# Moving the batched columns of one softmax half from GpSimd to VectorE in a 64-step recurrent attention kernel

## Chip, cores, metric

One core of a Trainium2 chip. The metric is the device time of one execution in microseconds (us). Engines: PE is the matrix engine (PEld its weight loads), DVE is VectorE, ACT is ScalarE, POOL is GpSimd.

## The reference, cut to what matters

A layer of attention with recurrent memory is followed by a gated MLP. The attention walks 64 segments of 32 rows; eight memory rows of one segment's output are the first rows of the next, so the segments are a chain:

```python
for s in range(n_seg):                        # 64
    h = jnp.concatenate([mem, xs], axis=1)    # 8 + 32 rows
    q, k, v = ...                             # 32 heads of 128
    scores = jnp.einsum('bhqe,bhke->bhqk', q, k) * scale
    scores = jnp.where(mask[None, None], scores, -1000000000.0)
    p = _softmax(scores, axis=-1)
    o = jnp.einsum('bhqk,bhke->bhqe', p, v)
    o = jnp.einsum('bhte,hed->btd', o, Wo)
    mem = o[:, :M, :].copy()
```

## The kernel before

Each step treats the 32 heads in two halves, b = 0 and 1. Per half, the exponentials E have 160 columns for the segment's keys and 64 "batched" columns for the last eight keys, whose keys and values were made ahead for 16 segments at once. R holds the reciprocal sums. Both groups of columns are multiplied by R, then go into the value product. The comments give the line numbers by which the profile names the instructions.

```python
def qx_copy(s):     # L574: batched queries of step s
    ...
    pool(lambda e: e.tensor_copy(out=dst, in_=src), reads=..., writes=[("QTe", 0), ("QTe", 1)])

def sm_ln(b):       # L626
    act(... func=ACT.Ln ..., writes=[("R", b)])
def sm_rcp(b):      # L630
    act(... func=ACT.Exp, scale=-1.0 ..., reads=[("R", b)], writes=[("R", b)])

def sm_norm(b):
    dve(lambda e: e.tensor_tensor(out=E_sb[:, b, 0:160], in0=R_sb[:, b, :], in1=E_sb[:, b, 0:160], op=ALU.mult),   # L634
        reads=[("R", b), ("E", b)], writes=[("E", b)])
    ev = E_sb[:, b, 160:224].rearrange("p (g q) -> p g q", q=16)
    rv = R_sb[:, b, :].rearrange("p (g q) -> p g q", q=40)[:, :, 0:16]
    pool(lambda e: e.tensor_tensor(out=ev, in0=rv, in1=ev, op=ALU.mult),                                           # L638
         reads=[("R", b), ("Ex", b)], writes=[("Ex", b)])

def PV_half(s, b):
    for g in range(4):
        for c in range(4):
            pe(...)     # L666: V x E,  reads=[("V", b, g), ("E", b)]
    for c in range(4):
        pe(...)         # L672: batched V x Ex, stop=True, reads=[("Vx", xb, b), ("Ex", b)]
...
# in a step, from the second half's softmax on
sm_norm(0); sm_sums(1); sm_ln(1); sm_rcp(1)
...
V_evac(1, "dve", (0, 2))      # L658
V_evac(1, "act", (2, 4))      # L656
sm_norm(1)
if s + 1 < NSEG: qx_copy(s + 1)
...                           # filler matmuls; even steps have one group more than odd ones
PV_half(s, 0)
PV_half(s, 1)
...                           # two groups of filler matmuls
cT_evac(...)                  # L686 on ACT, L688 on VectorE: out of PSUM, wait for L672
Wo(WOQ, OB, 0, OC)            # L701: output product, waits for cT_evac
```

Waits are derived from the `reads` and `writes` tokens. Instructions on PE take no waits on earlier PE instructions; every other engine also waits for itself where a token says so, and each GpSimd instruction waits for the one before it.

The softmax here doesn't subtract the row's maximum and nothing guards it: scores larger than these inputs give would overflow.

Of the kernel before, what the change touches and what calls it, by code (L numbers as in the profile page):

```python
# [10 lines left out]
ALU = mybir.AluOpType  # L11
# [167 lines left out]
def fast_path(nc, st, keep, A_x, A_mem0, A_Wq, A_Wk, A_Wv, A_Wo, A_seg_len, B_w_in, B_w_sp, B_b_sp, B_w_out, out):  # L179
# [118 lines left out]
    def dve(fn, **k):  # L298
        return em.add("dve", fn, **k)

    def pool(fn, **k):
        return em.add("pool", fn, **k)
# [330 lines left out]
    def sm_norm(b):  # L633
        dve(lambda e: e.tensor_tensor(out=E_sb[:, b, 0:160], in0=R_sb[:, b, :], in1=E_sb[:, b, 0:160], op=ALU.mult),  # L634
            reads=[("R", b), ("E", b)], writes=[("E", b)])
        ev = E_sb[:, b, 160:224].rearrange("p (g q) -> p g q", q=16)
        rv = R_sb[:, b, :].rearrange("p (g q) -> p g q", q=40)[:, :, 0:16]
        pool(lambda e: e.tensor_tensor(out=ev, in0=rv, in1=ev, op=ALU.mult),  # L638
             reads=[("R", b), ("Ex", b)], writes=[("Ex", b)])

    def V_half(s, b, gs, dc, first=0, last=3, held=False):
# [293 lines left out]
    for s in range(NSEG):  # L935
# [68 lines left out]
        V_half(s, 1, (0, 2), 1, 3, 0)  # L1004
        V_half(s, 1, (0, 2), 0, 3, 0)
        sm_norm(0)
        sm_sums(1)
        sm_ln(1)
# [4 lines left out]
# [3 lines that stand above are left out]
        if s + 1 < NSEG:  # L1016
            qx_copy(s + 1)
# [1041 lines left out]
```

## Time and profile before

| | before |
|---|---|
| time, median of 3 runs (range) | 852.48 us (852.42 to 853.62) |
| profiled run | 850.12 us, span 848.4 us, granted clock 0.999 |
| the 64-step scan | from 52 to about 673 us of the span |
| PE busy | 834.1 us, 98% |
| VectorE, GpSimd busy | 515.3 and 168.7 us |

The prediction below shows the lines themselves. A row of the page's groups reads: line, engine, operation, output<-inputs, count, busy us and mean ns, then idle time before it and what ended it. A timeline line reads: start us, duration us, engine, line, operation, and in brackets the idle time before it. I also used the trace's own records, which carry each start and end, and the moment of each semaphore update, in ns.

### The profile page before, as it was taken

How to read it: one execution, taken by the hardware profiler on the slowest of the kernel's cores; microseconds unless marked ns; L12 is line 12 of the kernel's file. 1: busy time of each engine (PE TensorE's matmuls, PEld its weight loads, DVE VectorE, ACT ScalarE, POOL GpSimd, SP SyncE). 2: the span in 40 equal slices, each digit the busy share in tenths (PEclk: the TensorE clock that was granted, in tenths of full speed). 3: DMA queues.
4: the chain of work that ended last, by engine and by line, in shares of the span. 5: the costliest groups of instructions: out<-in, count | busy, mean ns of one | idle time of the engine just before them, and what ended most of it. 6: DMA issues, size and time to landing. Idle time of an engine off the chain costs nothing.

```text
span 848.4 us, 46072 instructions
## 1 busy us (share of the span) xinstructions
PE 834.1 (98%) x22552; PEld 438.3 (52%) x19480; DVE 515.3 (61%) x1322; ACT 471.7 (56%) x1367; POOL 168.7 (20%) x425
## 2 busy tenths in 40 slices
PE   8889999999999999999999999999999999999998
PEld 8545555555545555555555555555555544444443
DVE  3456666676666666666766666666666664453443
ACT  3446666766667676667666666767666755300000
POOL 7312212121212122221222121122111232100000
PEclk9999999999999999999999999999999999999999
DMA  9972220222332221322222324242321690033001
GB/s 319 392 231 75 69 74 28 60 72 61 77 92 58 50 66 43 75 38 61 60 73 73 95 57 80 60 94 72 58 52 56 188 280 7 1 112 106 32 12 40
DMA packets 112920, 75.25 MB, mean 89 GB/s; under 512 B 70728, under 2 KB 98512, under 8 KB 112720
## 3 DMA queue, kind: packets, MB, share of 16 engines
q1 hardware_dynamic: 111504, 70.88, 30.2%
q8 instruction: 166, 2.72, 1.3%
q0 software_dynamic: 384, 1.05, 0.3%
q10 hardware_dynamic: 832, 0.33, 0.1%
q14 instruction: 34, 0.28, 0.1%
HBM read 39.46 MB, written 20.58 MB: 71 GB/s over the span
## 4 chain that ended last, share of the span: by engine, by line
PE 92%; SPq 5%; DMA 1%; issue 0%; DVE 0%; ACT 0%
PE f_ps L289 33%; PE f_ps L701 14%; PE f_ps L290 12%; PE f_ps L1172 11%; PE f_ps L751 3%; PE f_ps L666 3%; PE f_ps L1165 3%; PE f_ps L1248 3%; SPq L329 3%; PE f_ps L1129 3%; PE f_ps L498 2%; DMA f_arena<-in_A_Wo_dram 1%; SPq L825 1%; PE f_ps L595 1%; PE f_ps L615 1%; PE f_ps L672 1%
## 5 line engine op out<-in xcount | busy, mean ns | idle before, releaser
L289 PE MATMUL f_ps<-f_arena,f_hT 128*32 128x512 bf16 (+1 forms) x5632 | 359.7, 331 | 0.3
L289 PEld LDWEIGHTS f_ps<-f_arena,f_hT 128*32 128x32 bf16 x5632 | 133.1, 96 | 161.6 <-issue 69.8
L290 PE MATMUL f_ps<-f_arena,f_hT 128*32 128x512 bf16 (+1 forms) x2560 | 188.5, 315 | 0.0
L559 ACT ACTIVATE f_Tst<-f_ps 128x512 bf16<-128x512 f32 (+1 forms) x320 | 149.7, 510 | 57.6 <-PE f_ps L289 53.9
L701 PE MATMUL f_ps<-f_arena,f_cT 128*32 128x256 bf16 x4096 | 130.6, 274 | 0.9 <-DMA f_arena<-in_A_Wo_dram 0.6
L638 POOL TENSOR_TENSOR f_E_sb<-f_R_sb,f_E_sb 128x64 bf16<-128x64 f32 x128 | 57.0, 446 | 362.1 <-ACT f_R_sb L630 362.1
L567 DVE STREAM_TRANSPOSE f_QT<-f_Tst 128x256 uint32<-128x256 uint32 x128 | 57.1, 446 | 94.3 <-ACT f_Tst L559 94.3
L701 PEld LDWEIGHTS f_ps<-f_arena,f_cT 128*32 128x32 bf16 x4096 | 90.0, 94 | 37.1 <-ACT f_cT L686 23.2
L1172 PE MATMUL f_ps<-f_arena 128*128 128x512 bf16 x448 | 100.6, 379 | 0.0
L688 DVE TENSOR_SCALAR f_cT<-f_ps 128x160 bf16<-128x160 f32 x256 | 65.2, 318 | 35.2 <-PE f_ps L672 35.2
L713 ACT ACTIVATE f_part<-f_ps 128x256 bf16<-128x256 f32 x128 | 49.1, 383 | 57.7 <-PE f_ps L701 53.7
L658 DVE TENSOR_SCALAR f_V_sb<-f_ps 128x512 bf16<-128x512 f32 (+1 forms) x128 | 71.1, 555 | 13.6 <-PE f_ps L289 13.6
L686 ACT ACTIVATE f_cT<-f_ps 128x160 bf16<-128x160 f32 x256 | 57.1, 310 | 36.3 <-PE f_ps L672 36.3
L1172 PEld LDWEIGHTS f_ps<-f_arena 128*128 128x128 bf16 x448 | 43.8, 98 | 52.8
L567 DVE STREAM_TRANSPOSE f_KT<-f_Tst 128x128 uint32<-128x128 uint32 (+1 forms) x192 | 65.9, 356 | 2.8
L626 ACT ACTIVATE f_R_sb<-f_ps 128x160 f32<-128x160 f32 x128 | 38.9, 304 | 34.8 <-PE f_ps L290 34.8
L634 DVE TENSOR_TENSOR f_E_sb<-f_R_sb,f_E_sb 128x160 bf16<-128x160 f32 x128 | 41.7, 326 | 23.4 <-ACT f_R_sb L630 23.4
L1178 DVE TENSOR_TENSOR f_arena<-f_ps,f_arena 128x512 f32<-128x512 f32 x28 | 19.3, 690 | 54.4 <-PE f_ps L1172 52.4
L289 PE MATMUL f_ps<-f_arena,f_hTe 128*32 128x512 bf16 x640 | 48.8, 382 | 0.0
L608 ACT ACTIVATE f_E_sb<-f_ps 128x224 bf16<-128x224 f32 x128 | 45.9, 359 | 0.1
L751 PE MATMUL f_ps<-f_arena,f_cTx 128*32 128x512 bf16 x512 | 43.9, 379 | 0.5 <-issue 0.4
L630 ACT ACTIVATE f_R_sb<-f_R_sb 128x160 f32<-128x160 f32 x128 | 42.6, 332 | 2.0
(123 smaller groups left out, 1027.3 us busy)
## 6 DMA issues: line engine op xcount, KB each, us to landing
wT_d<-f_wst SPq DMA_DIRECT2D x32, 256.0 KB
f_arena<-wT_d SPq DMA_DIRECT2D x32, 256.0 KB
f_arena<-in_A_Wv_dram SPq DMA_DIRECT2D x4, 1024.0 KB
f_arena<-in_A_Wk_dram SPq DMA_DIRECT2D x4, 1024.0 KB
f_arena<-in_A_Wo_dram SPq DMA_DIRECT2D x4, 1024.0 KB
f_Vx<-vext_d SPq DMA_DIRECT2D x124, 32.0 KB
f_arena<-in_A_Wq_dram SPq DMA_DIRECT2D x3, 1024.0 KB
vext_d<-f_Vs SPq DMA_DIRECT2D x20, 128.0 KB
```

Of the source, the lines that this page charges most:

```text
L289: return e.matmul(out, lhsT=lhsT, rhs=rhs, start=start, stop=stop, skip_group_check=True, tile_position=pos)
L290: return e.add_instruction(mybir.InstMatmult(name=nc.get_next_instruction_name(), engine=mybir.EngineType.PE, ins=[e.lower_ap(rhs), e.lowe ...
L559: act(lambda e: e.activation(out=st_.rearrange("p (hp i r) -> p hp i r", i=32, r=2), in_=ps[:, bank, 0:64 * np_].rearrange("p (hp r i) -> ...
L567: dve(lambda e: e.transpose(out=dst, in_=src), reads=tok, writes=[(nm, b, k) for k in halves(b, p0, np_)])
L638: pool(lambda e: e.tensor_tensor(out=ev, in0=rv, in1=ev, op=ALU.mult), reads=[("R", b), ("Ex", b)], writes=[("Ex", b)])
L658: dve(lambda e: e.tensor_scalar(out=dst, in0=src, scalar1=VSC, scalar2=None, op0=ALU.mult), reads=[PB(bank)], writes=tok)
L686: act(lambda e: e.activation(out=dst, in_=src, func=ACT.Copy, scale=UNSC), reads=[PB(PVB[c])], writes=tok)
L688: dve(lambda e: e.tensor_scalar(out=dst, in0=src, scalar1=UNSC, scalar2=None, op0=ALU.mult), reads=[PB(PVB[c])], writes=tok)
L701: pe(lambda e, h=h, g=g, i=i, b=b, c=c: e.matmul(ps[32 * g:32 * g + 32, bank, 0:d1 - d0], lhsT=cTh[:, i, 8:40], rhs=w_o[:, h, d0:d1], star ...
L713: act(lambda e: e.activation(out=part[:, s % 8, d0:d1], in_=ps[:, bank, 0:d1 - d0], func=ACT.Copy), reads=[PB(bank)], writes=[("part", s % ...
L751: pe(lambda e, h=h, g=g, i=8 * qr + bg: e.matmul(ps[32 * g:32 * g + 32, WXB, :], lhsT=cTx[:, rb % 2, i, :], rhs=w_o[:, h, :], start=(i < 4 ...
L1172: pe(lambda e: e.matmul(ps[:, bank, 0:TB], lhsT=z2[:, sc, fb * 128:(fb + 1) * 128], rhs=wTb[tb % 2][:, :, sc, :], start=(sc == 0), stop=(s ...
```

## The change

The intent: take the batched columns' multiplication of the second half from the slower engine and put it on VectorE, right behind the other columns. GpSimd keeps those of the first half.

```diff
-        pool(lambda e: e.tensor_tensor(out=ev, in0=rv, in1=ev, op=ALU.mult),
+        (dve if b else pool)(lambda e: e.tensor_tensor(out=ev, in0=rv, in1=ev, op=ALU.mult),
              reads=[("R", b), ("Ex", b)], writes=[("Ex", b)])
```

## The prediction

> **What bounds the kernel now.** I read the page first, for the busiest engine and the chain that ended last.
>
> ```profile
> PE 834.1 (98%) x22552; PEld 438.3 (52%) x19480; DVE 515.3 (61%) x1322; ACT 471.7 (56%) x1367; POOL 168.7 (20%) x425
> ...
> PE 92%; SPq 5%; DMA 1%; issue 0%; DVE 0%; ACT 0%
> ...
> L638 POOL TENSOR_TENSOR f_E_sb<-f_R_sb,f_E_sb 128x64 bf16<-128x64 f32 x128 | 57.0, 446 | 362.1 <-ACT f_R_sb L630 362.1
> ...
> L634 DVE TENSOR_TENSOR f_E_sb<-f_R_sb,f_E_sb 128x160 bf16<-128x160 f32 x128 | 41.7, 326 | 23.4 <-ACT f_R_sb L630 23.4
> ```
>
> The matrix engine (PE) is busy 98% and carries 92% of the last chain. The scan over 64 segments runs from 52 to 671 us; each step (9.5 to 10 us) has two softmax halves. Each half is scaled by two multiplications (128 of each kind in all): 160 columns on VectorE (L634), 64 batched columns on GpSimd (L638). The change moves the second half's 64 L638 to VectorE. Everything therefore hangs on whether PE waits for that one instruction. Asked who waits for L638, the profile says nobody:
>
> ```profile
> L638 POOL TENSOR_TENSOR f_E_sb<-f_R_sb,f_E_sb x128: 440/446/450, 51.3 to 670.2; 128x64 bf16<-128x64 f32 x128
> ...
>   ACT f_R_sb L630: 362.1, 128
> who waited for it (us, times):
> ```
>
> I did not accept that: a weight load takes 90 ns and overlaps the next, so a wait shorter than this leaves no idle gap to attribute. The timeline of one odd step (37) shows it:
>
> ```profile
> 415.24 0.33 DVE L634 TENSOR_TENSOR f_E_sb<-f_R_sb,f_E_sb 128x160 bf16<-128x160 f32 x1 [0.16 <-ACT f_R_sb L630]
> 415.28 0.45 POOL L638 TENSOR_TENSOR f_E_sb<-f_R_sb,f_E_sb 128x64 bf16<-128x64 f32 x1 [0.38 <-ACT f_R_sb L630]
> ...
> 415.62 0.17 PEld L666 LDWEIGHTS f_ps<-f_E_sb,f_V_sb 32*128 32x128 bf16 x16
> ...
> 415.78 0.10 PEld L672 LDWEIGHTS f_ps<-f_E_sb,f_Vx 32*128 32x128 bf16 x4
> ...
> 415.79 0.40 POOL L574 COPY f_QT<-f_arena 128x256 bf16<-128x256 bf16 x1
> ...
> 416.02 0.70 ACT L686 ACTIVATE f_cT<-f_ps 128x160 bf16<-128x160 f32 x3 [0.54 <-PE f_ps L672]
> ...
> 416.37 0.20 PEld L701 LDWEIGHTS f_ps<-f_arena,f_cT 128*32 128x32 bf16 x8 [0.33 <-ACT f_cT L686]
> ```
>
> L666 is the value product of the second half (needs L634), L672 its batched part (needs L638). L638 ends at 415.73 and L672 starts at 415.78. Then ACT's L686 copies the result out, and L701, the output product, waits for it: the end of L672 is on PE's path.
>
> The view rounds to 10 ns, so I took start times, and the recorded moments of semaphore updates, from the trace's records for all 64 steps. Times are ns after the first L666 of the step, medians from step 4 on:
>
> | | L634 start, end | L638 end | L666 second half, first to last | L672 starts |
> |---|---|---|---|---|
> | odd steps | -51, 275 | 440 | 327 to 407 | 492 |
> | even steps | -266, 60 | 226 | 120 to 240 | 277 |
>
> L672 starts 51 to 52 ns after L638 in 62 of 64 steps (24 and 42 wait for the batched values' load instead). So PE's issue does wait for GpSimd. Is the finish of L672 also set by that? In the odd steps, 0 to 3 and 60 to 63 (36 steps) PE's update for L672 comes 267 to 269 ns after the end of L638, whatever else varies: GpSimd sets it. In the 28 even steps from 4 to 58 it comes 506 or 532 ns after the first L666 in nearly all, while L638's end wanders from 223 to 228: there both halves' matmuls run back to back, PE's own backlog sets the finish, and GpSimd does not. An even step (36):
>
> ```profile
> 405.55 0.45 POOL L638 TENSOR_TENSOR f_E_sb<-f_R_sb,f_E_sb 128x64 bf16<-128x64 f32 x1 [0.38 <-ACT f_R_sb L630]
> ...
> 405.89 0.21 PEld L666 LDWEIGHTS f_ps<-f_E_sb,f_V_sb 32*128 32x128 bf16 x16
> ...
> 406.05 0.10 PEld L672 LDWEIGHTS f_ps<-f_E_sb,f_Vx 32*128 32x128 bf16 x4
> ...
> 406.30 0.50 ACT L686 ACTIVATE f_cT<-f_ps 128x160 bf16<-128x160 f32 x2 [0.56 <-PE f_ps L672]
> ```
>
> Here L686 starts 250 ns after L672, against 240 in the odd step. In every step but the first, L701 starts 376 to 378 ns after that update, so what the update gains, L701 gains.
>
> **What the Trainium skill says.** "VectorE: DVE Perf Modes", section on the TRN2 errata, gives (N+151)/0.96 ns for an fp32 two-input operation. For 160 columns that is 324; the trace has 324 to 329, so I use it for 64 columns: 224 ns. The same page, "The DRAIN you can't avoid", says the next operation does not start until the pipe is empty; the trace differs: after L634 the next VectorE instruction (L658, 64 times) starts 241 to 244 ns after L634's start, 83 ns before its reported end. The measurement decides. "GPSIMD Engine Reference", section 8, says GpSimd shares its SBUF interfaces with VectorE and contends with its two-input instructions. In the trace L638 lies beside L634 128 times and L634 still takes its 324 to 329; no contention shows in this pair.
>
> **The change, part by part.**
> Removed: 64 L638 from GpSimd, 64 x 446 ns = 28.5 us; POOL busy falls from 168.7 to about 140.
> Added: 64 L638 on VectorE. The order of instructions of the changed kernel has each directly behind the second L634 with no wait of its own, and PE's L672 waits for VectorE where it waited for GpSimd; other engines are unchanged. 64 x 224 = 14.3 us, of which 83 ns each overlap L634, so VectorE's busy time rises by 64 x (224 - 83) = 9 us to about 524.
> On the path: the result is ready 242 + 224 = 466 ns after L634 starts, where GpSimd has it at 440 + 51 = 491. That is 25 ns earlier. The news travels equally fast: L666 starts 52 to 53 ns after L634 where it waits for VectorE, L672 51 to 52 after GpSimd.
> Worth: in 36 steps GpSimd set the finish; step 0 then waits for the Wo load, leaving 35. Floor in the odd steps: issue could be at 407 + 15 = 422, below the new 467. PE's backlog: 506 - 216 (L672's own latency in the odd steps) over 9 sets of four tiles is 32 ns a set, so the finish cannot come before 327 + 4 x 32 + 216 = 671, below the new 683. The 25 ns fit. 35 x 25 = 0.87 us. In the 28 even steps: nothing.
> Moved: L574, the copy of the next step's batched queries, stood behind the removed L638; it now follows the first half's L638, some 0.8 us earlier. Its reader is the next step's score product, 6 us later: no gain. In an odd step it will run from -321 to 75, beside the second L634.
> VectorE's next work, L688, waits for L672 and starts some 0.3 us after it; the added instruction ends before that.
>
> Sum: 852.48 - 0.87 = 851.6 us.
>
> **The rivals.**
> 1. Contention. L574 now overlaps L634 (second half) by some 126 ns, which it never did. If VectorE is held for part of that, L666 and L672 of the second half are late. For: the skill's sentence; and L638 beside L634 is weak evidence, since its reads may come after L634's. Against: no L634 was ever lengthened. If L634 grew by 60 ns, the 35 steps would lose 60 - 25 = 35 ns, +1.2 us, and even steps, where L634's end has about 8 ns of slack, up to 28 x 50 = 1.4 us: together 852.5 + 2.6 = 855 us.
> 2. The even steps gain too, if their finish follows the issue of L672 after all: 63 x 25 = 1.6 us, 850.9 us. Against: the constant 506.
> 3. The gain is lost: VectorE's second instruction starts later than 242 ns, or its short form costs more than 224. Only 25 ns are at stake, so 852.5; at 50 ns more than expected, +0.9 us, 853.4.
> 4. A VectorE bound: no. It is at 61%, and idle for the half microsecond before L688.
> 5. A wait for a load takes the place of the gain (steps 24 and 42 show one): it would eat single steps.
>
> **Range and chances.** The mechanisms span 850.9 to 855, the likely ones 851 to 853.4; three runs before lay between 852.42 and 853.62, and the profiled one at 850.12, so noise is about the size of the effect. Range 850.3 to 853.4. Two per cent is 17 us, 266 ns in each of 64 steps, more than either multiplication of the batched columns could return; nothing in the list comes near it. Faster by over 2%: 0.005; slower: 0.01; within: 0.985.
>
> **What would show it.** L638 on DVE x64 at about 224 ns, starting 242 after L634; L672 starting 466 + 52 = 518 ns after L634 starts in odd steps, where it was 543; even steps with an unchanged 506. L634 still 324 to 329 (rival 1 wrong) although L574 overlaps it. Wrong would be: L634 or L638 lengthened, or L672's update no longer 267 ns behind the multiplication in odd steps.

## The result, and the profile after

The changed kernel ran at a median of 852.74 us (851.15 to 854.45, 4 runs) against 853.05 (852.42 to 854.0, 4 runs) for the kernel before. The ratio is 0.9996 with a 95% interval of 0.9972 to 1.0019: the same. (A ratio is the mean time of one kernel's fast runs over that of the other's of the same rounds, so not quite the ratio of the medians.) The forecast 851.6 and its range hold. The interval is 4 us wide, though, and the forecast gain was 0.87 us, so the time alone says nothing of the mechanism. The traces do.

The page of the kernel after, busy time of the engines:

```profile
PE 835.4 (98%) x22545; PEld 440.2 (52%) x19480; DVE 524.1 (62%) x1386; ACT 471.6 (55%) x1367; POOL 140.0 (16%) x361
```

VectorE rose by 8.8 us (forecast 9, to 524) and GpSimd fell by 28.7 (forecast to 140). Asked for line L638, the profile of the kernel after gives minimum, median and maximum duration of both kinds:

```profile
L638 POOL TENSOR_TENSOR f_E_sb<-f_R_sb,f_E_sb x64: 438/444/448, 50.9 to 672.2; 128x64 bf16<-128x64 f32 x64
L638 DVE TENSOR_TENSOR f_E_sb<-f_R_sb,f_E_sb x64: 218/218/221, 51.9 to 673.2; 128x64 bf16<-128x64 f32 x64
```

The timeline of the same odd step (37) in the kernel after:

```profile
418.15 0.40 POOL L574 COPY f_QT<-f_arena 128x256 bf16<-128x256 bf16 x1
...
418.42 0.32 DVE L634 TENSOR_TENSOR f_E_sb<-f_R_sb,f_E_sb 128x160 bf16<-128x160 f32 x1 [0.16 <-ACT f_R_sb L630]
...
418.67 0.22 DVE L638 TENSOR_TENSOR f_E_sb<-f_R_sb,f_E_sb 128x64 bf16<-128x64 f32 x1
...
418.80 0.17 PEld L666 LDWEIGHTS f_ps<-f_E_sb,f_V_sb 32*128 32x128 bf16 x16
...
418.94 0.10 PEld L672 LDWEIGHTS f_ps<-f_E_sb,f_Vx 32*128 32x128 bf16 x4
...
419.18 0.89 ACT L686 ACTIVATE f_cT<-f_ps 128x160 bf16<-128x160 f32 x4 [0.52 <-PE f_ps L672]
...
419.53 0.66 PEld L701 LDWEIGHTS f_ps<-f_arena,f_cT 128*32 128x32 bf16 x24 [0.33 <-ACT f_cT L686]
```

The even step 36, whose lines before stand in the prediction, after the change:

```profile
408.54 0.22 DVE L638 TENSOR_TENSOR f_E_sb<-f_R_sb,f_E_sb 128x64 bf16<-128x64 f32 x1
...
408.57 0.17 PEld L666 LDWEIGHTS f_ps<-f_E_sb,f_V_sb 32*128 32x128 bf16 x16 [0.42 <-DVE f_V_sb L658]
...
408.82 0.12 PEld L672 LDWEIGHTS f_ps<-f_E_sb,f_Vx 32*128 32x128 bf16 x4
...
409.10 0.89 ACT L686 ACTIVATE f_cT<-f_ps 128x160 bf16<-128x160 f32 x4 [0.56 <-PE f_ps L672]
```

Here L686 starts 0.53 us after the step's first L666 (408.57), as it did before (405.77 to 406.30), though L672 is issued earlier: its finish has not moved. In the odd step, from the start of L634 to the start of L672 it was 415.24 to 415.78 before, 0.54 us; it is 418.42 to 418.94 now, 0.52. The copy L574 now stands before L634 and reaches into it. In ns after the first L666 of the step, medians:

| | odd: L638 ends | odd: L672 starts | odd: L672's update | even: L672 starts | even: L672's update |
|---|---|---|---|---|---|
| before | 440 | 491 | 707 | 277 | 507 or 532 |
| after | 410 | 463 | 679 | 250 | 507 or 532 |

The odd steps gained 28 ns at the end of the value product. In the even ones PE issues L672 27 ns earlier and finishes it at the same moment. (The even steps' two values: where the first half's L672 updates a semaphore too, the finish comes some 26 ns later, in both kernels.)

Where, then, do the microseconds of difference between single runs come from? I took each step's length (first L666 to the next step's first L666) for steps 1 to 62 in three traces with GpSimd at the second half's columns (the kernel before, its control, and the change turned round below) and three with VectorE there (the kernel after, its repeat, and the one with the copy held back), and each step's shortest over its three. Odd steps differ by a median of -28 ns, even ones by +2, and the sums by -0.75 us: 604.07 us against 603.33. The sum depends on which traces are taken: with any three of the five that have VectorE there (both halves on VectorE and the probe besides), it is -0.17 to -0.83 us, while the medians stay at -27 to -29 and +1 to +2 ns. Single traces lie above such sums by 2.2 to 4.8 us, in scattered pauses of 0.1 to 0.8 us at PE. Pauses of this kind are in all six traces, at other steps each time, and the kernel after had besides a PE pause of 2.5 us in step 0. I did not find their cause. They are several times the size of the effect.

### The profile page after: what moved, and what is told of

Read it like the earlier page. It is cut to its first block, busy times and chain, and to the rows that moved or that the text cites. A ratio compares the mean times of both kernels' runs of the same rounds, so it can differ in the third digit from the quotient of the medians.

```text
span 851.6 us, 46001 instructions
## 1 busy us (share of the span) xinstructions
PE 835.4 (98%) x22545; PEld 440.2 (52%) x19480; DVE 524.1 (62%) x1386; ACT 471.6 (55%) x1367; POOL 140.0 (16%) x361
## 4 chain that ended last, share of the span: by engine, by line
PE 91%; DMA 3%; SPq 3%; issue 1%; ACT 1%; DVE 0%; ACTq 0%
PE f_ps L289 33%; PE f_ps L701 14%; PE f_ps L290 12%; PE f_ps L1172 11%; PE f_ps L751 3%; PE f_ps L666 3%; PE f_ps L1165 3%; PE f_ps L1248 3%; PE f_ps L1129 2%; PE f_ps L498 2%; SPq L329 2%; DMA f_arena<-in_A_Wk_dram 2%; PE f_ps L595 1%; PE f_ps L615 1%; DMA f_arena<-in_B_w_in_dram 1%
## 5 line engine op out<-in xcount | busy, mean ns | idle before, releaser
L701 PE MATMUL f_ps<-f_arena,f_cT 128*32 128x256 bf16 x4096 | 132.8, 276 | 1.0 <-issue 0.6
L701 PEld LDWEIGHTS f_ps<-f_arena,f_cT 128*32 128x32 bf16 x4096 | 91.9, 95 | 39.1 <-ACT f_cT L686 22.3
L638 POOL TENSOR_TENSOR f_E_sb<-f_R_sb,f_E_sb 128x64 bf16<-128x64 f32 x64 | 28.4, 444 | 338.2 <-ACT f_R_sb L630 338.2
L658 DVE TENSOR_SCALAR f_V_sb<-f_ps 128x512 bf16<-128x512 f32 (+1 forms) x128 | 71.0, 555 | 13.6 <-PE f_ps L289 13.6
L686 ACT ACTIVATE f_cT<-f_ps 128x160 bf16<-128x160 f32 x256 | 57.1, 310 | 35.4 <-PE f_ps L672 35.4
L634 DVE TENSOR_TENSOR f_E_sb<-f_R_sb,f_E_sb 128x160 bf16<-128x160 f32 x128 | 41.7, 325 | 23.4 <-ACT f_R_sb L630 23.4
L709 POOL COPY f_cTx<-f_cT 128x256 bf16<-128x256 bf16 x64 | 25.6, 400 | 116.7 <-DVE f_cT L688 116.7
```

Of the source, the lines that this page charges most:

```text
L658: dve(lambda e: e.tensor_scalar(out=dst, in0=src, scalar1=VSC, scalar2=None, op0=ALU.mult), reads=[PB(bank)], writes=tok)
L686: act(lambda e: e.activation(out=dst, in_=src, func=ACT.Copy, scale=UNSC), reads=[PB(PVB[c])], writes=tok)
L701: pe(lambda e, h=h, g=g, i=i, b=b, c=c: e.matmul(ps[32 * g:32 * g + 32, bank, 0:d1 - d0], lhsT=cTh[:, i, 8:40], rhs=w_o[:, h, d0:d1], star ...
```

## The experiments

Theory: in odd steps, and in steps 0 to 3 and 60 to 63, the second half's L638 sets the end of L672, hence of the step; in the other even steps PE's own backlog does. The rivals: L638 is hidden everywhere; all steps are bound by it; the earlier copy L574 contends with VectorE. Later a further question came up: why L638 cost GpSimd 446 ns at all.

### Control, and the change again

The kernel before, unchanged, and the changed kernel, five rounds each on one chip.

> A control: the kernel before, unchanged (one comment added). Both theories: ratio 1.000, and the width of the interval says what change of time these runs can resolve at all. In the trace the per-step intervals repeat to about 2 ns: in odd steps the end of L672 (PE's semaphore update) 707 ns after the first L666 of the step, in even steps 507 or 532. The total may differ by 1 to 3 us by stalls that lie outside these intervals, because the trace of the changed kernel had a 2.5 us pause in step 0 and one more microsecond after the scan, neither of which the change touches.

> The changed kernel again, beside the control. My theory (GpSimd's multiplication set the end of L672 in 35 steps, 25 to 28 ns each): 0.9 to 1.0 us faster than before, ratio about 0.9989, probably inside the interval; in the trace odd steps 679 after the first L666 and even steps 507, as in its first trace. Rival 'hidden': odd steps 707 as before, and ratio 1.000. Rival 'all steps gain': even steps near 480.

Measured: the control against itself 0.9991 (0.9970 to 1.0013), the change 1.0003 (0.9984 to 1.0022). Steps of the control: odd 707, even 506. Of the change: odd 678, even 530 by median, a mixture of 507 and 532. So the steps repeat to about 2 ns, and total time cannot resolve 0.9 us even in five rounds: the control came out lower than the change. The rival "hidden" falls by the steps (odd 678, not 707), and "all steps" as well (even not near 480).

### One multiplication more on VectorE

```diff
+    scr = sb("scr", [128, 64], BF)...
     rv = ...
+    b and dve(lambda e: e.tensor_tensor(out=scr, in0=rv, in1=ev, op=ALU.mult), reads=[("R", b), ("Ex", b)], writes=["scr"])
     (dve if b else pool)(...)     # L638
```

> The changed kernel with one more multiplication of 128x64 (into an unused tile) on VectorE ahead of each second-half L638. My theory: L638 ends one start-to-start interval later, about 140 ns; in odd and edge steps the end of L672 moves by all of it (679 to about 819 ns after the first L666), in even steps only by what exceeds the slack of about 40 ns (507 to about 607). Sum 35 x 0.14 + 28 x 0.10 = 7.7 us, ratio to before about 1.008. Rival 'the batched columns are hidden anyway': no change, ratio 0.999 to 1.000. Rival 'even steps are bound by the multiplication as well': even steps move by 140, sum 8.8 us.

Measured: ratio 1.0134 (1.0103 to 1.0164), +11.4 us. Odd steps end at 937, which is +258 and not +140; even ones at 721, +214 from 507 (+189 in those that were at 532, hence the mean of 0.20 us below). The direction and the even steps' slack (258 - 214 = 44, expected 40) are as the theory has them, and the rivals "hidden" and "even steps as well" fall. The size I missed: L638 overwrites what the added instruction reads, so it waits for VectorE's own semaphore and starts 250 ns after the added one instead of some 140. By steps the sum is about 35 x 0.258 + 28 x 0.20 - 1.0 = 13.6 us against before; the total measured less, inside the interval.

### One multiplication more on GpSimd

The same extra line with `pool`, in the kernel before.

> The kernel before with one more multiplication of 128x64 (into an unused tile) on GpSimd ahead of each second-half L638. It costs 446 ns and the wait of GpSimd for itself, some 62, together 508. My theory: the end of L672 moves by 508 ns in the odd and edge steps (707 to 1215) and by about 495 in the even ones (507 to about 1002). Sum 35 x 0.508 + 28 x 0.495 = 31.6 us, ratio about 1.037. Rival 'hidden': GpSimd is busy 20% and nobody waits for it by the profile, so no change.

Measured: ratio 1.0227 (1.0197 to 1.0257), +19.4 us. Odd steps end at 1088 (+381), even ones at 877 (+370). An engine at 20% for which "nobody waits" costs 2.3% when it is 381 ns later. By steps the sum is 35 x 0.381 + 28 x 0.36 = 23.4 us, more than the interval of the time allows (16.8 to 21.9 us); steps 1 to 62 of this trace are 20.6 to 22.1 us longer than those of the three traces with GpSimd above. Where the rest was gained back is not shown. By line, the added instruction and L638 of this kernel:

```profile
L637 POOL TENSOR_TENSOR f_scr<-f_R_sb,f_E_sb x64: 388/445/446, 51.9 to 692.2; 128x64 bf16<-128x64 f32 x64
```

```profile
L638 POOL TENSOR_TENSOR f_E_sb<-f_R_sb,f_E_sb x128: 303/374/448, 51.1 to 692.7; 128x64 bf16<-128x64 f32 x128
...
who waited for it (us, times):
  PEld f_ps L672: 22.1, 62
```

Now that the wait is long enough to leave PE's loads idle, the profile names it: L672, 62 times. And the expected 508 ns failed for a reason worth following. The 128 L638 have two durations whose middle is the "median" 374: the first half's take 445, the second half's, which now follow the added one and stand clear of L634, 303. The same shape on the same engine costs 142 ns less.

### Both halves on VectorE, and the change turned round

```diff
-        (dve if b else pool)(lambda e: ...)
+        dve(lambda e: ...)                    # both halves
+        (pool if b else dve)(lambda e: ...)   # turned round
```

> Batched columns of both halves on VectorE. My theory: the first half's L638 is never on the path (its reader waits for the value evacuation long after), so this behaves as the changed kernel: odd steps 679 ns from the first L666 to the end of L672, even 507; ratio to before 0.999. Its first-half L638 pushes the value evacuation L658 back by about 140 ns, which has to show in no L634 start of the second half. Rival 'VectorE becomes the bound': L634 of the second half starts later than 32 ns after ACT's L630, steps grow by up to 140 ns, +9 us.

> The change turned round: the first half's batched columns on VectorE, the second half's stay on GpSimd. My theory: as the kernel before, odd steps 707 ns and L672's issue 51 ns after GpSimd, even 507: moving the first half is worth nothing. Rival 'any relief of GpSimd pays': odd steps shorter than 707.

Measured: both on VectorE, ratio 0.9998 (0.9971 to 1.0025), odd steps 679, even 507, and L634 of the second half still starts 31 to 33 ns after ACT's L630. Turned round (one look, 851.97 us): odd 709, even 508 or 532. The first half's multiplication is worth nothing in either place; only the second half's matters.

### The copy held back

```diff
-        (dve if b else pool)(lambda e: ...)
+        lastop["m"] = (dve if b else pool)(lambda e: ...)
...
-             writes=[("QTe", 0), ("QTe", 1)])
+             writes=[("QTe", 0), ("QTe", 1)], after=[lastop.get("m")])
```

> The changed kernel with GpSimd's copy L574 held back until the second-half L638 on VectorE is done, which is where it stood before. My theory: the earlier copy is worth nothing and costs nothing: odd steps 679, even 507, L634 and L638 on VectorE as long as in the changed kernel (326 and 218). Rival 'contention': with the copy out of the way L634 or L638 of the second half get shorter, and odd steps end before 679.

Measured (one look, 852.59 us): L574 starts 473 ns after the first L666 in odd steps (it was -322 in the changed kernel); odd steps 678, even 507, L634 and L638 as long as before. The earlier copy gains nothing and disturbs nothing.

### Half of the columns on each engine

```diff
+        b and dve(lambda e: e.tensor_tensor(out=ev[:, 0:2], in0=rv[:, 0:2], in1=ev[:, 0:2], ...), reads=[("R", b), ("Ex", b)], writes=[("Ex", b)])
-        pool(lambda e: e.tensor_tensor(out=ev, in0=rv, in1=ev, op=ALU.mult),
+        pool(lambda e: e.tensor_tensor(out=ev[:, 2 * b:4], in0=rv[:, 2 * b:4], in1=ev[:, 2 * b:4], op=ALU.mult),
-             reads=[("R", b), ("Ex", b)], writes=[("Ex", b)])
+             reads=[("R", b), ("Ey", b)], writes=[("Ey", b)])   # token Ey added where Ex is written and read
```

> The second half's 64 batched columns divided: 32 on VectorE behind L634, 32 on GpSimd beside it. By length VectorE's part ends 242 + about 185 = 427 ns after L634's start (466 predicted and 460 measured for all 64), GpSimd's at 45 + about 377 = 422. My theory: in odd steps the end of L672 then meets PE's own floor, which I worked out as 671 ns after the first L666, instead of falling to about 642: a gain of at most 8 ns on the changed kernel, even steps 507; ratio to before 0.998 to 0.999. Rival 'no floor there': odd steps near 642, another 35 x 0.037 = 1.3 us.

> The split kernel again. Its first ratio was 0.997 with an interval that just leaves out 1, though its steps end only 5 ns earlier than before in the odd and not at all in the even ones, worth 0.2 us. If the steps are right, the ratio is now 1.000 within the interval (the first was chance among stalls); if there is a gain outside the intervals I look at, it is 0.997 again.

Measured: odd steps 702 and 701 in the two traces, not 671; ratio 0.9970 (0.9943 to 0.9997) in three rounds, then 0.9996 (0.9984 to 1.0009) in five. The first interval, just clear of 1, was chance, as the steps had said (5 ns in 35 steps are 0.2 us). A floor at 671 was not reached, so it stays untested. What went wrong is VectorE's part, by line:

```profile
L637 DVE TENSOR_TENSOR f_E_sb<-f_R_sb,f_E_sb x64: 231/234/236, 51.6 to 670.9; 128x32 bf16<-128x32 f32 x64
```

32 columns took longer than the 218 ns of 64 columns in the changed kernel. The difference between the two: here GpSimd works beside it.

### The same part without GpSimd beside it

The second half's columns in two multiplications of 32, both on VectorE (the diff is that above with `dve` in both places for b = 1).

> The second half's batched columns in two multiplications of 32 columns, both on VectorE behind L634; GpSimd does nothing beside them. It measures a 32-column multiplication alone: in the split kernel it took 234 ns beside GpSimd, longer than the 218 of 64 columns alone in the changed kernel. If that was contention, it takes about [...]185 here; if 32 columns simply cost that, 234 again. End of L672: second part starts about 109 ns behind the first, ends 243 + 109 + 185 = 537 after L634's start, so odd steps 679 + 76 = 755, even about 540.

```profile
L637 DVE TENSOR_TENSOR f_E_sb<-f_R_sb,f_E_sb x64: 182/184/189, 51.9 to 674.5; 128x32 bf16<-128x32 f32 x64
```

Alone it takes 184, as expected from the length; beside GpSimd it took 234. Odd steps ended at 749 and even ones at 533 (expected 755 and 540); the even ones now follow the issue of L672 (316 + 216), past the backlog.

### A twin left on GpSimd

The changed kernel, with a multiplication of the removed one's shape and place on GpSimd, into an unused tile.

```diff
+        b and pool(lambda e: e.tensor_tensor(out=scr, in0=rv, in1=E_sb[:, 0, 160:224]..., op=ALU.mult), reads=[("R", b), ("Ex", 0)], writes=["scr"])
```

> The changed kernel with a multiplication of 128x64 left on GpSimd where the removed one stood (it reads the same R and the first half's columns, and writes an unused tile). Contention: L638 on VectorE, now beside it, grows from 218 by about the 49 ns seen in the split kernel, to some 267; odd steps end at 728 and not 679, so the change is worse than before (707); even steps at 507 to 515; sum against the changed kernel 35 x 0.049 = 1.7 us. No contention: 218, odd 679, even 507.

The profile's answer for L638 in this kernel, its VectorE line:

```profile
L638 DVE TENSOR_TENSOR f_E_sb<-f_R_sb,f_E_sb x64: 326/329/330, 52.0 to 676.5; 128x64 bf16<-128x64 f32 x64
```

L638 grew from 218 to 329, more than twice what I expected. Odd steps end at 790 (83 later than in the kernel before), even ones at 576; ratio 1.0041 (1.0026 to 1.0055), +3.5 us, clear of noise. L634 kept its 324 to 329. So the engines do contend, and the changed kernel escapes it only because no multiplication is left on GpSimd beside its L638. A rough fit of the two cases: in odd steps the twin ends at 438 and L638 at 520, 82 ns later; GpSimd's 32 columns in the split end at 379 and VectorE's part at 425, 46 later. The difference of 36 ns is near the 34 by which 64 columns alone exceed 32 (218 - 184), as if VectorE could read only once GpSimd was through. Two points make that an estimate, not a proof. It is also not shown what the two engines contend for: in each of these pairs both read the same tile, R, and no run puts the two multiplications side by side on different tiles.

### A probe of GpSimd with VectorE out of the way

Does GpSimd pay in the kernel before as well? There its L638 starts 44 to 53 ns after L634 and ends 488 to 495 ns after L634's start. In the kernel with the extra GpSimd multiplication one of them started 98 ns after L634, lasted only 388, and ended at 486 as well: the end is pinned to L634. The probe puts the same multiplication where VectorE only reads PSUM:

```diff
-        act(... func=ACT.Ln ...)                                                    # L626
+        op = act(... func=ACT.Ln ...); b or ... or pool(lambda e: e.tensor_tensor(out=scr, in0=R_sb[:, 1, :]..., in1=E_sb[:, 0, 160:224]..., op=ALU.mult), reads=[("R", 1), ("Ex", 0)], writes=["scr"], after=[op])
```

> A probe: the changed kernel with one more multiplication of 128x64 on GpSimd in each step but the first (the same shapes and types, into an unused tile), started by ACT's first L626, when VectorE works at L658, which reads PSUM alone, and no two-input VectorE instruction is near. Theory 'held by VectorE': GpSimd's L638 took 445 in every kernel because it stood beside L634; alone it costs the 303 that the second of the pair took in the kernel with the extra GpSimd multiplication, so the probe L627 takes about 303 and the first half's L638 still about 445. Rival 'first after idle': a GpSimd instruction after microseconds of idle costs 445 whatever VectorE does; then the probe takes 445, and the L638 some 60 ns behind it about 303. Odd steps 679, even 507 as in the changed kernel if the probe disturbs nothing.

Asked by line, the probe and, in a second answer, L638 of the same kernel:

```profile
L627 POOL TENSOR_TENSOR f_scr<-f_R_sb,f_E_sb x63: 305/307/310, 62.5 to 668.8; 128x64 bf16<-128x64 f32 x63
```

```profile
L638 POOL TENSOR_TENSOR f_E_sb<-f_R_sb,f_E_sb x64: 440/447/448, 51.7 to 669.2; 128x64 bf16<-128x64 f32 x64
```

The probe follows 2.7 us or more of GpSimd idleness and costs 307; L638, by median 0.16 us behind it, costs 447 beside L634. So idleness is not the reason; standing beside L634 is. (The probe also reads no tile that VectorE reads at that moment, so the open point above stays open.) Odd steps stay at 679 and even ones at 507. About 140 of the 446 ns that the change removed were the price of standing beside VectorE's L634.

No version beat both kernels: both halves on VectorE equal the change, the split is no better.

## Why the prediction was right, point by point

- **PE waits for L638 though the profile names no waiter.** Right. In the kernels before and after, L672 starts 51 to 58 ns behind L638 (but for two or three steps in which it waits for something else), and the profile names the wait as soon as it is long (381 ns more on GpSimd).
- **25 ns earlier.** 28 measured: VectorE's L638 ends 461 ns after L634's start, not 466, because it lasts 218 and not the 224 estimated by the formula; L672 follows it by 53 and not 52 ns, so 28 of the 30 arrive. Its start 242 ns after L634's held (241 to 244).
- **35 steps gain, 28 even ones do not.** Right: medians -28 and +2 ns; the even steps' constant 507 stayed although L672 was issued 27 ns earlier. Their slack was measured as 44 ns with the added VectorE multiplication (69 in the steps that end at 532).
- **0.87 us in all.** By steps 35 x 28 = 0.98 us, by the sums of shortest steps 0.75 (0.17 to 0.83 with other traces). The total time cannot show it: unchanged code against itself gave 0.9991.
- **Rival 1, the copy L574 against L634.** Rightly given a small part: L634 stayed at 324 to 329, and holding the copy back changed nothing. But my reading "no contention shows in this pair" of L638 beside L634 was wrong. I looked only at VectorE's duration. The contention was there, and GpSimd paid it: 446 instead of 307 ns. It did not spoil the number because I took GpSimd's 446 from the trace, contention included.
- **Rivals 3 to 5.** Nothing grew, VectorE did not become a bound (62%), and waits for loads stayed single.

## What to carry to other kernels

Whether an instruction is on the path is read from how constant the interval behind it is over many steps, not from the list of waiters: a wait shorter than an overlapping weight load (91 ns here) leaves no idle time to list. A short idle time is left out as well: in the twin kernel PE's loads stood idle for 74 ns before L672 in odd steps, and the profile named L672 once; with 224 ns (one VectorE multiplication more) it named it 62 times. When two engines work side by side, compare each one's duration with and without the other; the loser may be the engine one is not looking at. And where the forecast effect is a quarter of the noise of a run, compare steps, not totals.

## What the Trainium skill lacked or had wrong

- "GPSIMD Engine Reference", section 8, says that GpSimd and VectorE contend where VectorE has two SBUF inputs, without an amount. Here the second to start of two multiplications paid: GpSimd's 128x64 took 445 to 447 ns beside an earlier L634 and 307 alone, while L634 kept 324 to 329; VectorE's 128x64 took 329 beside an earlier GpSimd one and 218 alone, its 128x32 234 and 184. Beside GpSimd's copy L574, which in odd steps had started 0.27 us earlier, L634 paid nothing.
- The same page, section 3.1, gives GpSimd's cost of this two-input operation at 2048 elements; for 64 columns the runs show 303 to 310 ns.
- "VectorE: DVE Perf Modes", "The DRAIN you can't avoid", measured a semaphore after each of eight VectorE copies as costing nothing extra. Here L638 with a wait for VectorE's own semaphore started 34 ns after the end of the one before it, and without a wait 83 ns before that end.
- The same page's errata formula (N+151)/0.96, which it calls exact at 512 and 2048 columns, gives 324, 224 and 191 ns for 160, 64 and 32; the runs show 324 to 329, 218 and 184.
